# Attention and a two-layer product on one core: bias product for two pairs, bias rows and weights moved in the DMA queues, second matmul from the end of the eighth slot

## Chip, cores and metric

One core of one Trainium2 chip. The time is the device time of one execution in microseconds. Ratios are the mean time of one kernel's fast runs over the mean of the other's fast runs of the same rounds, so not quite the ratio of the medians quoted beside them. For a program on one core, "slow" says only that a run was over 1.5% above the fastest of the same kernel; such runs are named where they matter.

## The reference, cut to what matters

```python
batch, n_heads, seq, head_dim = 8, 8, 576, 64
scores = q @ k.T / sqrt(64)
cum    = cumsum(maximum(s, 0))                      # along the sequence
bias   = minimum(-(cum[:, None] - cum[None, :]), 0)
attn   = softmax(where(causal, -1e9, scores + bias))
x      = concat_heads(attn @ v)                     # 4608 x 512
h      = x @ w_in                                   # 512 -> 2048
out    = (h * clip(h + 3, 0, 6) / 6) @ w_out        # 2048 -> 512
```

## The kernel before

Two heads make a pair, and one turn of the main loop (a **slot**, counted from 0, so the eighth slot is slot 7) handles one of the 32 pairs. From slot 4 on, groups of four matmuls of the two-layer product ("1": first layer, "2": second layer) fill TensorE's time between the parts of the attention. The plan of the first slots is fixed; a dot is an empty place:

```python
NROW = 1                                    # pairs whose bias comes by extra matmuls
plan = list("1.1.1.1" + "1.1.1.1." + "1.1.1.12" + "12121.12")     # slots 4, 5, 6, 7
```

The bias of pair 0 comes by extra matmuls (`picked` holds one selected row set per head). For pairs after that, four bias rows are appended to q and k by a small DMA (`load_aug`), and from pair 8 on also a staircase of constants (`set_stair`, two GpSimd copies). The queue order on GpSimd and SyncE is the order of this loop (cut):

```python
    load_aug(1, nc.sync)
    for i in range(2): load_qk(2, i)        # SyncE, into raws[2]
    load_v(1, nc.sync)
    load_aug(2, nc.sync)
    for i in range(2): load_qk(3, i)
    load_aug(3, nc.sync)
    load_v(2, nc.sync)
    cast_qk(1); cast_v(0); cast_qk(2)       # GpSimd
    ...
    I, U = load_w_in, load_w_out            # GpSimd's DMA queue
    for p in range(NP):
        if NPE <= p + 3 < NP:               # NPE = 9
            for i in range(2): load_qk(p + 3, i)                  # SyncE
        if NPROD <= p + 3 < NPROD + NQK:    # p = 5 .. 8
            set_stair((p + 3) % NQK, nc.gpsimd.tensor_copy)
        if p and p + 3 < NP:
            load_aug(p + 3, nc.gpsimd)
        ...
        elif p:                             # p >= 4
            qk_ahead()                      # GpSimd loads q, k of pairs 7, 8
            if NPE <= p + 2 < NP:
                cast_qk(p + 2)              # GpSimd
                crossbar_qk(p + 2)          # SyncE: DMA transpose into jt
            for fn, c in {4: ((I, 2),), 5: ((U, 0), (U, 1)), 6: ((I, 3),),
                          7: ((U, 2), (U, 3)),
                          8: ((U, 4), (U, 5), (U, 6), (U, 7))}.get(p, ()):
                fn(c)
            if nxt: cast_v(p + 1)           # GpSimd
        if p + 3 < NP: load_v(p + 3, nc.sync)
        # then TensorE, ScalarE, VectorE work of pair p; VectorE spreads jt of pair p + 1
```

The softmax here doesn't subtract the row's maximum and nothing guards it: scores larger than these inputs give would overflow.

## Time and profile before

| | before |
|---|---|
| median of the runs | 380.63 us (379.78 to 381.44) |
| span of the profiled run, mean granted clock | 378.9 us, 0.973 |
| TensorE busy | 354.6 us |
| slot 4, slot 8, slot 9 begin (first score matmul) | 33.01, 71.91, 88.85 us |
| from slot 9 to the end | 290.0 us |

How to read it: TensorE is full from slot 9 on, so the question is only when slot 9 begins. Slot 8 alone lasts 16.9 us, while slots 9 to 11 last some 9.2 us each. The lines that show this stand in the prediction below. (The prediction has slot 9 at 89.02, a time from the chain of work; TensorE's timeline has its first score matmul at 88.85.)

### The profile page before, as it was taken

The page shows a single profiled execution, that of the slowest core. Times are in us where ns is not written, and L with a number is a line of the kernel's source. Part 1 is how long each engine was busy: PE and PEld are TensorE (multiplying, and loading weights), DVE is VectorE, ACT ScalarE, POOL GpSimd, SP SyncE. Part 2 cuts the span into 40 slices and gives each one's busy share as a digit, 9 for nine tenths or more (in the row PEclk, how much of TensorE's full clock was granted, in tenths as well). Part 3 has the DMA queues.
Part 4 walks back from the last instruction along what each step waited for, and adds up shares of the span by engine and source line. Part 5 has one row for each costly group of instructions (what it writes and reads, how often), then busy time and mean ns, then how long its engine had stood idle before and what let it go on. Part 6 is the DMA issues. An engine that isn't in the chain of part 4 may idle for free.

```text
span 378.9 us, 7705 instructions
## 1 busy us (share of the span) xinstructions
PE 354.6 (94%) x2895; PEld 196.1 (52%) x2895; DVE 245.1 (65%) x547; ACT 217.6 (57%) x379; POOL 128.6 (34%) x223
## 2 busy tenths in 40 slices
PE   7879996659998899999999999999999999999996
PEld 3656663335554555555555555555555544444442
DVE  7755984517689776767676767676766644535541
ACT  4646983425665766666666666666666534343420
POOL 5578885523547533333333333333200000000000
PEclk9988999859999999999999999999999999999999
DMA  9799999395998799998999979797921101001102
GB/s 184 145 170 199 213 218 193 49 212 103 222 166 170 156 185 175 189 156 190 156 171 177 209 135 228 129 206 154 197 54 45 47 28 57 36 20 57 57 22 88
DMA packets 158141, 52.76 MB, mean 139 GB/s; under 512 B 146824, under 2 KB 153016, under 8 KB 158104
## 3 DMA queue, kind: packets, MB, share of 16 engines
q1 hardware_dynamic: 148680, 45.64, 60.8%
q0 software_dynamic: 8160, 6.20, 10.6%
q10 hardware_dynamic: 1264, 0.44, 0.6%
q8 instruction: 22, 0.36, 0.4%
q14 instruction: 15, 0.12, 0.1%
HBM read 37.36 MB, written 9.44 MB: 124 GB/s over the span
## 4 chain that ended last, share of the span: by engine, by line
PE 76%; DMA 6%; POOL 6%; issue 5%; DVE 4%; ACT 1%; SPq 1%; POOLq 0%
PE po L466 31%; PE ph L439 29%; PE O L373 6%; PE S L303 6%; PE S L292 3%; DMA w_in_sb<-in_moe_w_in_dram 2%; DMA raw<-in_k_dram 2%; DMA w_out_sb<-in_moe_w_out_dram 2%; POOL qk L140 1%; POOL qk L568 1%; DVE qk L208 1%; DVE gT L455 1%; POOL tok L180 1%; DMA raw<-in_q_dram 1%; POOL va L184 1%
## 5 line engine op out<-in xcount | busy, mean ns | idle before, releaser
L466 PE MATMUL po<-w_out_sb,gT 128*128 128x512 f16 x576 | 147.3, 380 | 9.7 <-DMA w_out_sb<-in_moe_w_out_dram 9.7
L455 DVE SCALAR_TENSOR_TENSOR gT<-tr,ph 128x512 f16<-128x512 f32 x144 | 98.7, 685 | 86.8 <-ACT tr L454 85.7
L439 PE MATMUL ph<-xT,w_in_sb 128*128 128x512 f16 x576 | 149.4, 381 | 1.5 <-DMA w_in_sb<-in_moe_w_in_dram 1.0
L322 ACT ACTIVATE P<-S 128x512 f16<-128x512 f32 x192 | 112.1, 594 | 59.6 <-PE S L292 30.8
L454 ACT ACTIVATE tr<-ph,bias 128x512 f32<-128x512 f32 x144 | 99.0, 687 | 81.9 <-PE ph L439 73.3
L466 PEld LDWEIGHTS <-gT 128*128 128x128 f16 x576 | 50.3, 98 | 56.1 <-issue 11.2
L439 PEld LDWEIGHTS <-w_in_sb 128*128 128x128 f16 x576 | 51.5, 98 | 45.5 <-DMA w_in_sb<-in_moe_w_in_dram 1.1
L140 POOL DMA_DIRECT2D qk<-rows_of x56 | 32.6, 583 | 112.4 <-PE Sc L344 52.8
L303 PE MATMUL S<-qk 68*128 68x448 f16 (+3 forms) x256 | 50.9, 281 | 0.2 <-ACT P L322 0.2
L373 PE MATMUL O<-va,P 128*128 128x65 f16 x896 | 49.3, 196 | 1.1 <-POOL va L184 1.1
L373 PEld LDWEIGHTS <-P 128*128 128x128 f16 x896 | 41.1, 99 | 15.4 <-issue 1.9
L180 POOL CAST tok<-raw 128x576 f16<-128x576 f32 x52 | 33.7, 677 | 14.4 <-DMA raw<-in_q_dram 8.5
L303 PEld LDWEIGHTS <-qk 68*128 68x128 f16 x256 | 24.3, 101 | 25.3 <-issue 2.1
L208 DVE COPY qk<-jt 64x768 f16<-64x768 f16 x92 | 34.6, 376 | 1.3
L396 DVE TENSOR_TENSOR x<-O,rl 128x320 f16<-128x320 f32 x64 | 31.5, 492 | 2.2
L292 PEld LDWEIGHTS <-qk 128*128 128x128 f16 (+1 forms) x256 | 20.2, 100 | 17.8 <-issue 2.9
L475 DVE TENSOR_SCALAR ob<-po 128x512 f32<-128x512 f32 x36 | 24.6, 683 | 7.0 <-PE po L466 7.0
L292 PE MATMUL S<-qk 128*128 128x128 f16 (+1 forms) x256 | 26.0, 223 | 3.1 <-DVE qk L208 2.3
L324 DVE TENSOR_TENSOR P<-P,shut 128x512 f16<-128x512 f16 x48 | 21.4, 445 | 5.4 <-ACT P L322 5.3
L395 DVE RECIPROCAL rl<-O 128x5 f32<-128x5 f32 x64 | 12.1, 189 | 15.1 <-PE Sc L344 8.2
L184 POOL CAST va<-vraw 128x512 f16<-128x512 f32 x32 | 20.1, 628 | 3.2 <-PE O L373 2.6
L238 DVE COPY qk<-pt 64x576 f16<-64x576 f16 x15 | 12.0, 803 | 6.4 <-ACT qk L238 5.1
(69 smaller groups left out, 170.4 us busy)
## 6 DMA issues: line engine op xcount, KB each, us to landing
out_dram<-ob SPq DMA_DIRECT2D x36, 256.0 KB, 2.7
vraw<-in_v_dram SPq DMA_DIRECT2D x64, 128.0 KB, 6.3
raw<-in_q_dram SPq DMA_DIRECT2D x27, 288.0 KB, 4.2
raw<-in_k_dram SPq DMA_DIRECT2D x26, 288.0 KB, 5.9
w_in_sb<-in_moe_w_in_dram POOLq DMA_DIRECT2D x4, 512.0 KB, 8.6
w_out_sb<-in_moe_w_out_dram POOLq DMA_DIRECT2D x8, 256.0 KB, 6.5
vraw<-in_v_dram SPq DMA_DIRECT2D x32, 32.0 KB, 3.0
qk<-rows_of POOLq DMA_DIRECT2D x56, 9.0 KB, 3.2
```

Of the source, the lines that this page charges most:

```text
L140: eng.dma_start(out=qks[p % NQK][64:68, hh, :, 64 * hh : 64 * hh + SEQ], in_=rows_of[g // 32].rearrange("(r g) i t -> g r i t", g=32)[g % ...
L180: copy(out=toks[p][:, c], in_=raws[p % NRAW][:, c])
L208: copies[par](out=qk[0:64, :, i, 128 * par : 128 * par + 256 * n].rearrange("p h (s two c) -> p h s two c", two=2, c=128)[:, :, :, 0, :], ...
L292: mm(S[:, c], lhsT=kT[rows, c], rhs=qT[rows, c], start=(j == 0 and not by_product), stop=(j == 3),)
L303: mm(S[:, c : c + w], lhsT=kT[0:68, 128 * j : 128 * (j + 1)], rhs=qT[0:68, 128 * (j + 1) : SEQ], start=(c == 0), stop=(c != 0 and p >= NROW),)
L322: nc.scalar.activation(out=pt[:, c], in_=S, func=AF.Exp, scale=0.125)
L373: mm(o[:, i, :], lhsT=lhsT, rhs=va[:, hh, j, 0:65], **kw)
L396: nc.vector.tensor_tensor(out=X[p][:, :, hh, :], in0=o[:, :, 0:64], in1=rl.to_broadcast([128, 5, 64]), op=ALU.mult,)
L439: mm(ph, lhsT=w_in_sb[:, kc, ft * 128 : (ft + 1) * 128], rhs=xT[:, kc, n * 512 : (n + 1) * 512], start=(kc == 0), stop=(kc == NKC - 1),)
L454: nc.scalar.activation(out=tr, in_=ph, func=AF.Relu, bias=bias3[:, 0:1])
L455: nc.vector.scalar_tensor_tensor(out=gTs[n][:, ft, :], in0=tr, scalar=6.0, in1=ph, op0=ALU.min, op1=ALU.mult)
L466: mm(po, lhsT=gTs[n][:, ft, t4 * 128 : (t4 + 1) * 128], rhs=w_out_sb[:, ft, :], start=(ft == 0), stop=(ft == NFT - 1),)
```

## The change

The intent is to get the weights of the second layer in before TensorE wants them, and to want them a little later. Cut to its core:

```diff
-    NROW = 1
+    NROW = 2
-    picked = keep("picked", [128, 2, SEQ], F16)
+    picked = w_out_sb.rearrange("p f j -> p (f j)")[:, 0 : 2 * NROW * SEQ].rearrange(...)
-    plan = list("1.1.1.1" + "1.1.1.1." + "1.1.1.12" + "12121.12")
+    plan = list("1.1.1.1" + "1.1.1.1." + "1.1.1.1." + "1.1.1212")
+    (rows 64 to 67 of pair 1's q and k zeroed by two ScalarE multiplications)
     # front
-    load_aug(1, nc.sync)          # also load_aug(2), load_aug(3)
     cast_qk(1)
+    load_aug(2, nc.gpsimd)
     cast_v(0)
     cast_qk(2)
+    load_aug(3, nc.gpsimd)
+    cast_v(1)
     # loop
-        if NPROD <= p + 3 < NPROD + NQK:
-            set_stair((p + 3) % NQK, nc.gpsimd.tensor_copy)
-        if p and p + 3 < NP:
-            load_aug(p + 3, nc.gpsimd)
                 4: ((I, 2),),
-                5: ((U, 0), (U, 1)),
-                6: ((I, 3),),
-                7: ((U, 2), (U, 3)),
-                8: ((U, 4), (U, 5), (U, 6), (U, 7)),
+                5: ((I, 3),),
+                6: ((U, 0), (U, 1), (U, 2), (U, 3)),
+                7: ((U, 4), (U, 5), (U, 6), (U, 7)),
             ...
+            if NPROD <= p + 2 < NPROD + NQK:
+                set_stair((p + 2) % NQK, nc.gpsimd.tensor_copy)
+            if p + 2 < NP:
+                load_aug(p + 2, nc.gpsimd)
     # slots 2, 3: load_aug(4), load_aug(5) go last; cast_v(3) one slot later, cast_v(4) ahead of qk_ahead()
     # bias of the second half of the heads: each step one slot later
```

Below, "front" means the bias product for pair 1 and all that moves ahead of the loop; "plan" the later second matmuls; "weights" all the rest in the loop. Slots are counted from 0 here; the "slot eight" in the name of the prediction's step 4 is the eighth one, slot 7.

More of the change, by code (lines that the diff above doesn't have):

```diff
@@ L95 @@
     sel = keep("sel", [128, 4], F32)
-    picked = keep("picked", [128, 2, SEQ], F16)
+    picked = w_out_sb.rearrange("p f j -> p (f j)")[:, 0 : 2 * NROW * SEQ].rearrange(
+        "p (g t) -> p g t", t=SEQ
+    )
     toks = {}
@@ L539 @@
     load_v(0, nc.sync)
-    for i in range(NROW):
-        fill(nc.gpsimd, qks[i][64:68, :, :, :], 0.0)
     fill(nc.gpsimd, ident, 0.0)
@@ L591 @@
     fill(nc.gpsimd, rows_of[0][:, 1, SEQ:640], 0.0)
+    fill(nc.gpsimd, qks[0][64:68, :, :, :], 0.0)
+    for hh in range(2):
+        nc.scalar.mul(
+            out=qks[1][64:68, hh, :, 64 * hh : 64 * hh + 640],
+            in_=rows_of[0][64:68, 0, None, :].to_broadcast([4, 2, 640]),
+            mul=0.0,
+        )
     for i in range(NQK):
@@ L665 @@
     load_v(1, nc.sync)
-    load_aug(2, nc.sync)
     for i in range(2):
         load_qk(3, i)
-    load_aug(3, nc.sync)
     load_v(2, nc.sync)
     cast_qk(1)
+    load_aug(2, nc.gpsimd)
     cast_v(0)
     cast_qk(2)
+    load_aug(3, nc.gpsimd)
+    cast_v(1)
     for i in range(2):
@@ L694 @@
         if p == 1:
-            cast_v(1)
             cast_qk(3)
@@ L700 @@
             qk_ahead()
+            load_aug(4, nc.gpsimd)
+        elif p == 3:
             cast_v(3)
-        elif p == 3:
             load_w_in(1)
+            cast_v(4)
             qk_ahead()
-            cast_v(4)
+            load_aug(5, nc.gpsimd)
         elif p:
@@ L724 @@
             nc.sync.dma_start(out=stair_sb, in_=stair_dram.ap())
-        if p == 9:
+        if p == 10:
             load_s(1, (nc.sync,) * 4)
             fill(nc.gpsimd, rows_of[1][:, 0, :], 1.0)
-        if p == 10:
+        if p == 11:
             cum1(1, nc.gpsimd)
-        if p == 11:
+        if p == 12:
             cum2(1)
             nc.gpsimd.tensor_copy(out=rows_of[1][0:32, 0, 0:SEQ], in_=C["c"][0:32])
-        if p == 12:
+        if p == 13:
             cum3(1, nc.gpsimd)
             cum4(1, nc.gpsimd)
-        if p == 12:
+        if p == 13:
             cum5(1, nc.gpsimd)
```

## The prediction

> **What bounds the kernel now.** I read the page's engine shares and slices first, then TensorE's waits, then the chain that ended last, and then the timelines of TensorE and GpSimd where the chain leaves TensorE. The shares and slices:
>
> ```profile
> PE 354.6 (94%) x2895; PEld 196.1 (52%) x2895; DVE 245.1 (65%) x547; ACT 217.6 (57%) x379; POOL 128.6 (34%) x223
> ...
> PE   7879996659998899999999999999999999999996
> ...
> PEclk9988999859999999999999999999999999999999
> DMA  9799999395998799998999979797921101001102
> GB/s 184 145 170 199 213 218 193 49 212 103 222 166 170 156 185 175 189 156 190 156 171 177 209 135 228 129 206 154 197 54 45 47 28 57 36 20 57 57 22 88
> ```
>
> The reader should see that TensorE is full from slice 10 on (about 90 us) and has nothing left to give there. Nearly all its idle time (378.9 - 354.6 = 24.3 us) lies in the first 90 us, together with two stretches of lowered clock. The eighth slice moves only 49 GB/s while its neighbours move 193 and 212: DMA stood empty there although the kernel was short of weights. Who was waited for, by TensorE between 60 and 90 us:
>
> ```profile
> PE po L466 <- DMA w_out_sb<-in_moe_w_out_dram: 9.7, 4, 5.9
> ```
>
> and why those weights came late, in GpSimd's timeline:
>
> ```profile
> 58.62 1.47 POOL L156 DMA_DIRECT2D w_out_sb<-in_moe_w_out_dram  x2
> ...
> 62.46 1.25 POOL L568 COPY qk<-stair_sb 64x1280 f16<-64x1280 f16 x1 [1.52 <-PE Sc L344]
> 70.20 1.25 POOL L568 COPY qk<-stair_sb 64x1280 f16<-64x1280 f16 x1 [6.48 <-PE S L303]
> 71.40 1.20 POOL L140 DMA_DIRECT2D qk<-rows_of  x2
> 72.64 1.37 POOL L180 CAST tok<-raw 128x576 f16<-128x576 f32 x2
> 73.96 2.88 POOL L156 DMA_DIRECT2D w_out_sb<-in_moe_w_out_dram  x4
> ```
>
> This is a loop. The last four weight transfers stand behind a staircase copy in GpSimd's in-order queue; the copy waits for TensorE to finish with a pair's buffer; TensorE itself stands waiting for earlier weights (third and fourth transfers, issued at 58.62). So the last weights start at 73.96 and TensorE stands again. TensorE's timeline, with the early wait as well:
>
> ```profile
> 23.74 0.57 PE L222 MATMUL pt<-ident,tok 128*128 128x128 f16 x5 [1.51 <-POOL tok L180]
> ...
> 65.35 0.65 PE L466 MATMUL po<-w_out_sb,gT 128*128 128x512 f16 x2 [1.82 <-DMA w_out_sb<-in_moe_w_out_dram]
> ...
> 78.25 1.01 PE L466 MATMUL po<-w_out_sb,gT 128*128 128x512 f16 x2 [5.94 <-DMA w_out_sb<-in_moe_w_out_dram]
> 80.66 1.01 PE L466 MATMUL po<-w_out_sb,gT 128*128 128x512 f16 x2 [1.40 <-DMA w_out_sb<-in_moe_w_out_dram]
> ```
>
> **What the Trainium skill says.** "TensorE: Matmul & The Clock Gate", Part 1, says that idleness drops TensorE to half clock until some 3.4 us of work have passed. The trace agrees in kind: after 23.74 the starts of successive 512-column matmuls go from 0.22 to 0.43 us apart until 31.6; the same from 65.8 to 69.2 and from 80.7 to 86.7. So a removed wait is worth more than itself. "DMA: Bandwidth & Descriptors", section "Issuing engines are not separate DMA queues", says that transfers of all issuers interleave on the same 16 engines, so issuing weights earlier gives no extra bandwidth, only fills holes; the 49 GB/s slice is such a hole. "SBUF — State Buffer", the list of practical consequences under who interferes with whom, says that a VectorE copy in a two-port mode and a GpSimd instruction lock each other out. The trace agrees: the two query/key copies of VectorE that take 0.67 us at 104.67 take 3.30 us at 115.15, beside GpSimd's bias casts. That matters for the part of the change that shifts the second bias by one slot.
>
> **The change part by part.** A slot is one head pair; slot 4 begins at 33.01, slot 7 at 56.72, slot 8 at 71.91, slot 9 at 89.02 (the starts of each pair's first score matmuls).
>
> (1) Bias product for a second pair. Pair 1 gets its bias by extra matmuls instead of by rows sent by DMA. For pair 0 these cost three groups of 0.22 us a head (spacing of the starts at 13.43, 14.09 and 14.78 to the next group) plus 0.03 in the corner: 0.69 a head, 1.38 for pair 1, all on TensorE: **+1.4 us**. The two further picks on VectorE (0.36 each) end near 11.9, and VectorE was idle 0.98 before its next copy at 12.18: nothing. Two ScalarE multiplications of 1280 columns fall between the table load's end at 3.43 and the first cast at 5.93, which waited 2.5 us for its data. From the 0.67 us of a 576-column cast and 0.70 of a 768-column copy I estimate 1.1 to 1.3 each, so they end at 5.7 to 6.0: at most 0.1. The picked rows now lie in the second weights' memory; the first such weights arrive 20 us after their last use: nothing.
>
> (2) Bias rows leave SyncE's queue. SyncE stood from 7.81 to 9.27 waiting for the rows, and later again, so pair 2's load started at 10.62 and pair 3's at 15.39. Now they can go at about 7.9 and 11.4. GpSimd's cast of pair 3 waited 2.81 us for k and ended at 23.68, which gave TensorE's 1.51 wait; by bytes (about 3.3 MB ahead of it at some 175 GB/s) it should land near 18 to 19. Two waits for value casts (0.64 at 19.42, 0.49 at 26.25) go as well, since those casts move ahead. **-2.6 us**, and the half-clock stretch from 25.0 to 31.6 (6.6 less 0.5 idle, half of it lost) **-3.1 us**. The row transfers now cost GpSimd 1.2 us per pair between casts, where it has room.
>
> (3) Weights ahead of staircases, staircases one slot later. The staircase for pair p+2 goes into a buffer whose pair ended a slot before, so the 6.48 us stall of GpSimd goes and the loop is cut. By adding GpSimd's durations in the new order I expect the last first-matmul weights near 35 (they were at 50.3), second weights 0 to 3 at 37 to 40 (44.3 and 58.6), 4 to 7 at 46 to 49 (74.0). With 6.5 to 9 us of landing these are there by 58. This removes 9.74 of waits for second weights, 0.99 for first weights (at 58.57), and the half-clock losses of 65.8 to 69.2 (1.7) and 80.66 to 86.69 (0.4 in the two matmuls, 2.5 after): **-15.3 us**.
>
> (4) Second matmul from the end of slot eight. Walking through the plan and the rules that follow it, two groups of four matmuls (0.86 us each) leave slots 6 and 7 and fall into slot 8, where first matmuls are not ready and four places were empty. From slot 9 to the end both kernels do the same groups in the same places, with 12 left for the tail. Same work: 0, but weights are wanted some 2 us later.
>
> (5) Second half's bias one slot later. The waits of 1.75, 0.33, 0.42 and 0.22 between 116 and 128 may move by a slot, but I see no reason for them to go or grow much: 0.
>
> Sum: 380.6 + 1.4 - 2.6 - 3.1 - 15.3 = 361.0.
>
> **The rivals.** *DMA becomes the bound of the front.* Up to the last second weights (80.6) the core moved some 13.85 MB; its best stretch (48.6 to 56.7) ran at 221 GB/s at a share of 1.24. About 13.0 MB of that is needed by them or before. With 3.5 MB in the first 20 us and 215 GB/s after, the end is at 20 + 9.5/0.215 = 64 us. TensorE, by my new starts (slot 4 at 29, slot 8 at 61, slot 9 at 69), wants weights 4 and 5 near 65 and 6 and 7 near 68. That is a tie, not a margin. For it: DMA is already full from 27 to 56. Against it: the order is weights first, and v and raw loads are three pairs ahead. If it wins, waits of 3 to 8 us with some half clock come back: 365 to 370.
>
> *A wait on the first weights or rows takes the place of the early one.* First weights chunk 0 would be issued at 20 and land at 28.6 by the median of 8.6; slot 4 wants them at 29.9. The rows of pair 4 (issued near 22.3, 5.5 us landing early on) are wanted at 29.2, the q and k of pair 4 at 26.5. Each is within 1 or 2 us. Likely cost 0 to 3, up to 5 with a clock drop: 361 to 366.
>
> *The gain is given back later*, through collision of the shifted bias work on GpSimd with VectorE's copies, or since slots 12 and 13 have seven empty places: 0 to 3 us more.
>
> I add **2.5 us** to the sum for the first two together: **363.5 us**.
>
> **Range and chances.** The low end, 358.5, is the sum with no new wait and a little from the waits near 116 to 128. The high end, 371, is the DMA rival in full with an early wait. For not being faster by over 2% the time must stay above 373.0, so more than 12 of the 22.4 us gained gross would have to return; the change moves transfers only to earlier places in time and adds 1.4 us of work, so I give that 7 in 100: faster 0.93, same 0.06, slower 0.01.
>
> **What would show it right or wrong.** Right: second-weight transfers all issued before 52; TensorE's wait for them under 1 us; no 49 GB/s hole; clock above 0.98 (0.973 before); TensorE idle near 12 us and busy near 348; slot 9 starting near 69 to 72. Step 2 is wrong if TensorE still waits for a token cast near 21 or its clock falls before 32. Step 3 is wrong if GpSimd waits several us elsewhere ahead of the weights, say for a landing of v or raw. If DMA is the bound, weights are issued early but land over 12 us later. Step 4 is wrong if the number of second-matmul groups in the tail is not 12. The prediction fails altogether if a new wait over 5 us stands on TensorE before 90 us.

## The result, and the profile after

The changed kernel takes 368.8 us in median (366.3 to 369.8, 4 runs) against 381.0 of the kernel before (the three runs above and one of 384.1); the ratio is 0.966 (0.958 to 0.973). Predicted were 363.5, with 358.5 to 371 as the range. So the direction and the range held, and 5.3 us of the predicted gain did not come. The page of the profiled run, its lines that answer to those of before:

```profile
PE 351.6 (96%) x2913; PEld 194.1 (53%) x2913; DVE 251.0 (68%) x549; ACT 219.4 (60%) x381; POOL 133.7 (36%) x227
...
PE   8997999599998999999999999999999999999995
...
PEclk9999999899998999999999999999999999999999
DMA  9999999998898687989799979797521101101111
GB/s 183 211 203 212 205 193 161 172 214 184 194 183 175 154 190 167 189 136 211 160 192 181 189 165 185 169 191 159 123 77 20 57 2 57 57 2 58 57 57 60
```

The hole of 49 GB/s is gone, and the DMA engines are full from the first slice to the ninth. TensorE has one deep dip left, in the eighth slice, and a shallow one in the fourth. Whom it waited for up to 95 us (total, times, longest):

```profile
PE O L375 <- DVE x L398: 4.0, 1, 4.0
...
PE S L294 <- DMA qk<-rows_of: 0.8, 1, 0.8
```

No wait for second weights remains. In place of 9.7 us there is one wait of 4.0, put down to a VectorE instruction. VectorE's timeline shows what that instruction stood behind, and the chain that ended last shows the way back (start, length, what):

```profile
63.39 0.69 DVE L326 TENSOR_TENSOR P<-P,shut 128x512 f16<-128x512 f16 x1
69.22 0.66 DVE L210 COPY qk<-jt 64x768 f16<-64x768 f16 x2 [5.14 <-DMA jt<-tok]
69.80 0.18 DVE L397 RECIPROCAL rl<-O 128x5 f32<-128x5 f32 x1
70.02 0.49 DVE L398 TENSOR_TENSOR x<-O,rl 128x320 f16<-128x320 f32 x1
```

```profile
35.56 18.75 DMA raw<-in_q_dram
54.31 0.05 issue
54.36 1.28 POOL tok L182 x2
55.64 0.02 issue
55.66 13.54 DMA jt<-tok
```

Read from the top: the q of pair 9 was asked for at 35.56 and took 18.75 us to land, GpSimd cast it at 54.36, SyncE issued its DMA transpose at 55.66, and this took 13.54 us more. VectorE stood for the transposed tile from 64.08 to 69.22, and the normalisation behind it in its queue (L397, L398), which frees what TensorE needs next, came at 69.80 and 70.02. So the wait has two ingredients: a late transpose, and VectorE's order, in which the copies for pair 9 stand ahead of the normalisation of pair 7. Only the first was worked on below. With the two swapped, the normalisation need not have waited, and the tile that landed at 69.20 would have been copied out by about 70.6 (two pairs of copies, 0.66 us a pair: an estimate from these lines), ahead of the 70.97 at which slot 9 begins in the fastest profile below. No run tests this. GpSimd issued the last four weight transfers in the same microsecond as the transpose, since they too stood behind the cast:

```profile
42.08 2.88 POOL L158 DMA_DIRECT2D w_out_sb<-in_moe_w_out_dram  x4 [1.75 <-DMA qk<-rows_of]
...
54.36 1.27 POOL L182 CAST tok<-raw 128x576 f16<-128x576 f32 x2 [4.90 <-DMA raw<-in_q_dram]
55.58 2.88 POOL L158 DMA_DIRECT2D w_out_sb<-in_moe_w_out_dram  x4
```

Slot by slot, from the first score matmul of each pair:

| begin of | before | predicted | after |
|---|---|---|---|
| slot 4 | 33.01 | 29 | 28.67 |
| slot 8 | 71.91 | 61 | 61.89 |
| slot 9 | 88.85 | 69 | 75.81 |
| end, counted from slot 9 | 290.0 | as before | 290.8 |

All but one entry fit within 1 us. The shortfall is slot 8: it lasts 13.9 us where the sum had some 8. Its row in the table of stretches (stretch, length, then busy time and count for TensorE, weight loads, VectorE, ScalarE, GpSimd; clock, DMA share, GB/s) is this for the kernel before (cut at 89.02), then for the changed one:

```profile
71.91:89.02 17.11, 9.57 (x73) 5.68 (x72) 6.64 (x17) 4.22 (x8) 7.98 (x14) 0.70 0.78 133
```

```profile
61.89:75.81 13.92, 9.79 (x79) 5.23 (x77) 6.08 (x17) 4.37 (x8) 9.85 (x15) 0.88 1.22 161
```

DMA share went from 0.78 to 1.22 (it adds up the times of all packets, so it passes 1 where they overlap). Before, the engines had idle time in this slot; after, transfers lie on top of each other. It is not bytes alone: this slot moves 161 GB/s, while slot 9 of the same run moves 221 at a share of 0.99.

### The profile page after: what moved, and what is told of

It is laid out like the page before. It is cut to its first block, busy times and chain, and to the rows that moved or that the text cites. A ratio compares the mean times of both kernels' runs of the same rounds, so it can differ in the third digit from the quotient of the medians.

```text
span 366.6 us, 7736 instructions
## 1 busy us (share of the span) xinstructions
PE 351.6 (96%) x2913; PEld 194.1 (53%) x2913; DVE 251.0 (68%) x549; ACT 219.4 (60%) x381; POOL 133.7 (36%) x227
## 4 chain that ended last, share of the span: by engine, by line
PE 77%; DMA 12%; DVE 5%; POOL 2%; issue 1%; SPq 1%; ACT 1%; POOLq 0%; DVEq 0%; ACTq 0%
PE po L468 32%; PE ph L441 30%; PE O L375 6%; PE S L305 6%; DMA raw<-in_q_dram 5%; DMA jt<-tok 4%; PE S L294 3%; DMA vraw<-in_v_dram 2%; DMA raw<-in_k_dram 2%; DVE qk L210 1%; DVE gT L457 1%; DVE c L623 1%; POOL tok L114 1%; POOL tok L182 1%; SPq L134 0%
## 5 line engine op out<-in xcount | busy, mean ns | idle before, releaser
L182 POOL CAST tok<-raw 128x576 f16<-128x576 f32 x52 | 36.7, 710 | 107.6 <-DMA raw<-in_q_dram 98.2
L375 PE MATMUL O<-va,P 128*128 128x65 f16 x896 | 48.4, 194 | 4.0 <-DVE x L398 4.0
L305 PE MATMUL S<-qk 68*128 68x448 f16 (+3 forms) x256 | 49.5, 274 | 0.2
L375 PEld LDWEIGHTS <-P 128*128 128x128 f16 x896 | 40.1, 98 | 18.1 <-DVE x L398 4.3
L210 DVE COPY qk<-jt 64x768 f16<-64x768 f16 x92 | 38.2, 415 | 6.5 <-DMA jt<-tok 5.1
L142 POOL DMA_DIRECT2D qk<-rows_of x60 | 35.2, 589 | 1.4 <-DMA w_in_sb<-in_moe_w_in_dram 1.4
L398 DVE TENSOR_TENSOR x<-O,rl 128x320 f16<-128x320 f32 x64 | 31.5, 492 | 2.4 <-DVE rl L397 0.2
L326 DVE TENSOR_TENSOR P<-P,shut 128x512 f16<-128x512 f16 x48 | 22.3, 465 | 4.5 <-ACT P L324 4.4
L397 DVE RECIPROCAL rl<-O 128x5 f32<-128x5 f32 x64 | 12.0, 188 | 7.2 <-PE O L375 7.1
```

Of the source, the lines that this page charges most:

```text
L142: eng.dma_start(out=qks[p % NQK][64:68, hh, :, 64 * hh : 64 * hh + SEQ], in_=rows_of[g // 32].rearrange("(r g) i t -> g r i t", g=32)[g % ...
L182: copy(out=toks[p][:, c], in_=raws[p % NRAW][:, c])
L210: copies[par](out=qk[0:64, :, i, 128 * par : 128 * par + 256 * n].rearrange("p h (s two c) -> p h s two c", two=2, c=128)[:, :, :, 0, :], ...
L305: mm(S[:, c : c + w], lhsT=kT[0:68, 128 * j : 128 * (j + 1)], rhs=qT[0:68, 128 * (j + 1) : SEQ], start=(c == 0), stop=(c != 0 and p >= NROW),)
L375: mm(o[:, i, :], lhsT=lhsT, rhs=va[:, hh, j, 0:65], **kw)
L398: nc.vector.tensor_tensor(out=X[p][:, :, hh, :], in0=o[:, :, 0:64], in1=rl.to_broadcast([128, 5, 64]), op=ALU.mult,)
```

## The experiments

Two questions: which part brought the 12 us, and what is the 4 us wait that remains made of? Each run was timed beside the kernel before on the same chip. All gave correct results. By the 2% rule the verdict is "same" for d_front_only and "unclear" for d_plan_only and d_front_plan_only, "faster" for the rest; every interval lies below 1. The table collects the runs of the first question, with the begin of slot 9 in each profile and the waits of TensorE for second weights.

| run | parts of the change in it | median us | ratio to before (95%) | slot 9 | wait for second weights |
|---|---|---|---|---|---|
| before | none | 380.63 | 1 | 88.85 | 9.7 |
| d_front_only | front | 377.81 | 0.988 (0.984 to 0.991) | 84.95 | 10.6 |
| d_plan_only | plan | 374.84 | 0.981 (0.976 to 0.986) | 81.98 | 4.7 |
| d_weights_only | weights | 371.61 | 0.971 (0.965 to 0.976) | 80.70 | 4.4 |
| d_front_plan_only | front, plan | 371.53 | 0.975 (0.969 to 0.981) | 77.99 | 5.0 |
| d_front_undone | plan, weights | 370.85 | 0.968 (0.961 to 0.975) | (slow profile) | |
| d_plan_old | front, weights | 368.89 | 0.966 (0.959 to 0.972) | 75.63 | none |
| changed kernel, again | all | 369.04 | 0.968 (0.964 to 0.971) | 75.01 | none |

### Undoing one part: d_front_undone, d_front_plan_only, d_plan_old

d_front_undone puts the front back: `NROW = 1`, `load_aug(1..3, nc.sync)`, `cast_v(1)` in slot 1, the rest as changed.

> The changed kernel with its front put back: bias product for pair 0 only, bias rows of pairs 1 to 3 sent by SyncE, value cast of pair 1 in slot 1. Theory A (the changed kernel is held in slot 8 by the late transpose of pair 9, which landed at 69.2 us after a chain of transfers, not of TensorE work): TensorE comes to slot 8 some 3 to 4 us later and waits that much less there, so 368 to 371 us. Theory B (the parts add up as the prediction summed them): the front was worth 4.3 us, so 372.5 to 374 us with a wait of some 4 us still in slot 8.

Measured 370.85 (367.3 to 373.5; its profile fell in a slow run and is not used). The ratio, 0.968 (0.961 to 0.975), cannot be told from that of the changed kernel (0.966 and 0.968). A loss of 4.3 us would have given about 0.977, just beyond the interval's end, so theory A fits better. With the other two parts there, the front brought 0 to 1 us as measured; by the two intervals, a loss of up to some 3 us against the control is not excluded.

d_front_plan_only is the kernel before with the front and the plan; weights and staircases stay in the old order.

> The kernel before with only the new front and the new plan of second matmuls; weights and staircases stand in the old order. If the loop of weights, staircase and TensorE decides when TensorE gets past slot 8, the front's 4.3 us (7.1 before the product's 1.4 and so on) mostly vanish in longer waits for second weights: 378 to 381 us, waits for second weights 8 to 12 us. If parts add up: 375 to 377 us, waits for second weights about 9.7 us less 1 to 2 for the later start.

Measured 371.53, ratio 0.975: some 4 us better than even the additive expectation, which had given the plan nothing. TensorE waits half as long for second weights although their order is the old one:

```profile
PE po L468 <- DMA w_out_sb<-in_moe_w_out_dram: 5.0, 2, 3.2
```

d_plan_old is the changed kernel with the one line of the plan put back.

```diff
-    plan = list("1.1.1.1" + "1.1.1.1." + "1.1.1.1." + "1.1.1212")
+    plan = list("1.1.1.1" + "1.1.1.1." + "1.1.1.12" + "12121.12")
```

> The changed kernel with the old plan (second matmuls from the end of slot 6). Second weights 0 to 3 were issued at 42.1 to 45.0 and land within 11 us, so by 54 to 56, while the old plan wants them from 51.5 on. Theory A: up to 2 us of new wait for weights in slots 6 and 7, which the wait in slot 8 gives back, so 368 to 370 us. Rival: the waits add to the slot-8 wait with another clock drop, 371 to 374 us.

Measured 368.89, ratio 0.966, the same as the changed kernel. No wait for weights came up in slots 6 and 7; the only large one is again slot 8's, 3.4 us. So the plan is worth nothing measurable when front and weights are there, and something large when the weights are in the old order. That asked for each part alone.

### Each part alone: d_plan_only, d_front_only, d_weights_only

> The kernel before with only the new plan of second matmuls. Theory D (the loop of weights, staircase and TensorE can be cut in more than one place, so the parts overlap): with no second matmul in slot 7 that wants the late weights 2 and 3, the waits of 0.58 and 1.82 us and the half clock after them go, TensorE frees the staircase's buffer some 5 us earlier and the last weights are issued near 68 instead of 74: 374 to 377 us. Prediction's step 4 (the plan is worth nothing by itself): 380 to 382 us.

Measured 374.84, ratio 0.981: the expectation of overlapping parts. One line of Python is worth 7 us of 381 by itself. The last four weight transfers go out at 68.97 instead of 73.96, with not one GpSimd instruction moved:

```profile
68.97 2.89 POOL L156 DMA_DIRECT2D w_out_sb<-in_moe_w_out_dram  x4
```

> The kernel before with only the new front. Theory D: the front shifts the whole loop earlier by its own 4 us, so 376 to 378 us with the waits for second weights near 9 us as before. If the loop were tied to the arrival of weights alone: 380 to 381 us with longer waits.

Measured 377.81, ratio 0.988, as expected: slot 9 begins 3.9 us earlier, and the waits for second weights stay:

```profile
PE po L468 <- DMA w_out_sb<-in_moe_w_out_dram: 10.6, 4, 5.8
```

> The kernel before with only the new order of weights, staircases, bias rows and second bias. Theory D: it cuts the loop by itself, so it takes most of the gain: 369 to 372 us, with up to 2 us of waits for second weights since the old plan wants them early. If the parts add up (front 4.3 us): 373 to 374 us.

Measured 371.61, ratio 0.971, within the expected 369 to 372, with a wait of 4.4 us (up to 2 had been expected). Alone the three parts gain some 5, 7 and 11 us, 23 together (1 minus the ratio, times 381); combined they gain 12 to 13. The loop that the prediction found can be cut at TensorE's end (ask later, so that TensorE frees the staircase's buffer sooner) or at GpSimd's end (send the weights first). Either cut takes most of what the other would.

### What the remaining wait is made of: e_raw9_early, after_again, e_u_ahead, e_raw9_slot5, e_both

e_raw9_early asks for q and k of pair 9 two slots sooner; their buffer had been free since 19.4 us.

```diff
-        if NPE <= p + 3 < NP:
+        if NPE < p + 3 < NP:
             for i in range(2):
                 load_qk(p + 3, i)
+        if p == 4:
+            for i in range(2):
+                load_qk(NPE, i)
```

> The changed kernel with the q and k of pair 9 loaded by SyncE at the start of slot 4 instead of slot 6 (same bytes, earlier in the queue). Theory A (order): they took 18.8 us to land at 54.3; asked for before v of pairs 7 and 8 they land by 45, the cast, the last second weights and the transpose follow some 6 us earlier, the wait of 4 us in slot 8 and its half clock (1.8 us) go: 362.5 to 365 us. Rival C (bandwidth: the front of the kernel is bound by bytes or packets whatever their order): the wait moves to another load and the time stays within 367 to 370 us.

Measured 362.5, 363.8, 365.3 and 369.9 us (the last counted slow), ratio of the fast runs 0.953 (0.947 to 0.958): the expected time. In the profiled run TensorE has no wait over 1.2 us anywhere and slot 9 begins at 70.97. But the way there was not the one expected. The cast of pair 9 and the weights came not earlier but 2.5 us later, since GpSimd now stood for v of pair 7, which had been put behind:

```profile
52.00 0.61 POOL L186 CAST va<-vraw 128x512 f16<-128x512 f32 x1 [6.99 <-DMA vraw<-in_v_dram]
...
56.82 1.27 POOL L182 CAST tok<-raw 128x576 f16<-128x576 f32 x2
58.03 2.88 POOL L158 DMA_DIRECT2D w_out_sb<-in_moe_w_out_dram  x4
```

What differs is the transpose. It was issued at 58.12, again beside the weights, and no transpose of this run up to 90 us took over 6.1 us, where the changed kernel's took up to 13.5 (the last line of the view of the tile jt: least, median and most from issue to landing, first the changed kernel, then this run):

```profile
DMA to landing us min/median/max: 5.3/5.6/13.5
```

```profile
DMA to landing us min/median/max: 4.7/5.6/6.1
```

So the gain goes with a fast transpose and not with an earlier cast, and the weights in the same microsecond are not enough to make it slow. With the slow run counted in, the mean ratio would still be 0.957. To see whether the weights or SyncE's own loads made the transpose slow, four more ran on one chip with five rounds: the changed kernel as a control, and three orders. The early load itself was not among them.

> The changed kernel unaltered, as a control beside the three below on the same chip: 366 to 370 us, ratio to before near 0.966, the wait of 3 to 4 us in slot 8 for the transpose of pair 9 in the profile.

The control gave 369.04 (367.7 to 370.1), ratio 0.968, with a wait of 3.4 us in slot 8 and the transpose again slow (11.8 us).

e_u_ahead sends the last four weights ahead of pair 9's cast:

```diff
+            if p == 7:
+                for c in range(4, 8):
+                    load_w_out(c)
             if NPE <= p + 2 < NP:
                 cast_qk(p + 2)
                 crossbar_qk(p + 2)
-                7: ((U, 4), (U, 5), (U, 6), (U, 7)),
```

> The changed kernel with the last four second-weight transfers ahead of the cast of pair 9 on GpSimd (they waited behind it for pair 9's load until 55.6; now issued near 49.5). Theory W (pair 9's transpose took 13.5 us to land because these weights were issued in the same microsecond): it lands within 7 us of its issue near 57, the wait goes, 363 to 365 us. Theory Q (it stood behind SyncE's own backlog, v of pair 8 and q, k of pair 10 issued just before it): it still takes 10 us or more, and pair 9's load is delayed further by the weights; 367 to 370 us.

Measured 363.8, 365.4, 368.5, 369.4, 369.5 and 369.9, median 368.98: no clear gain (the ratio of 0.960 counts only the three fastest, since the others lie 1.5% above the best). Two of the six runs were as fast as the early load's (clock 0.998 and 0.995), as one of the early load's was slow (0.990), so the wait may come and go between executions; one execution of each is profiled. In it the transpose was fast, 6.2 us (no transpose up to 90 us took over 7.0). But pair 9's k now landed later, and the transpose could only be issued at 60.24:

```profile
50.04 2.90 POOL L158 DMA_DIRECT2D w_out_sb<-in_moe_w_out_dram  x4
...
58.11 0.67 POOL L182 CAST tok<-raw 128x576 f16<-128x576 f32 x1 [3.82 <-DMA raw<-in_k_dram]
```

In its profiled run 2.8 us of wait remained in slot 8. What the transpose gained, the load before it lost.

The eight fast profiles that have the "weights" part can be compared in this one transfer, the transpose of pair 9. It took 11.8 to 14.1 us in six of them (changed kernel twice, d_plan_old, d_weights_only, and e_raw9_slot5 and e_raw9_pair1rows below). In each of the six, SyncE had finished issuing k of pair 10 at most 0.6 us before, and the four weights were issued within 2 us of the transpose. It took 6.0 in the early load (k of pair 10 issued 3.2 us before, weights beside it) and 6.2 in e_u_ahead (k just before, weights 10 us before). So in these runs a slow transpose goes with both neighbours at once and with neither alone. With one run for each exception this is a pattern and not a shown cause.

> The early load of pair 9 at the start of slot 5 instead of slot 4, so behind v of pair 7 and ahead of v of pair 8. GpSimd's 7 us wait for v of pair 7 should go, the cast of pair 9 come near 49 to 52 and the last weights follow: 362 to 365 us, as with slot 4. If the load needs the full three transfers' head start, its cast stays past 54 and the wait in slot 8 stays over 2 us: 366 to 369 us.

Measured 370.68 (367.7 to 372.1), ratio 0.973: no gain, as the second expectation had it, and slower than its 366 to 369. GpSimd stood 4.26 us for k of pair 9, cast it at 53.66, and the wait in slot 8 was 4.6:

```profile
53.66 0.67 POOL L182 CAST tok<-raw 128x576 f16<-128x576 f32 x1 [4.26 <-DMA raw<-in_k_dram]
```

> The early load of pair 9 in slot 4 and the weights ahead of its cast. If the value cast of pair 7, which GpSimd waited 7 us for with the early load, stands behind the weights no more, nothing on TensorE changes, since no wait of TensorE hung on it: 362 to 365 us, as with the early load alone. If the weights issued near 56 now meet the transfers of v for pair 7 and of pair 10: 365 to 368 us.

Measured 367.4 to 373.2, median 371.53, ratio 0.970: worse than the early load alone, outside the expected 362 to 365 us. Its profile fell in a slow run, so where it waited is not told from it.

What follows: between slots 4 and 8 of the changed kernel (28.67 to 61.89) the DMA share lies at 1.13 to 1.26 and the rate at 178 to 209 GB/s, so a transfer that is moved ahead puts others back. Of four ways to reorder the same bytes, three left the time within 1% of the changed kernel's; in two of these GpSimd's wait for k of pair 9 took the place of what was saved, and for e_both it is not known. The fourth, the early load in slot 4, was faster in its one set of rounds (0.953, up to 0.958, against 0.968, from 0.964, of the control and 0.966, from 0.958, of the changed kernel's first set) and is the fastest version here; it was not run a second time, and e_both, which contains it, was not fast. Whether 364 us would hold on another chip is open.

### What the bias product for pair 1 is worth: e_raw9_pair1rows

The early-load kernel, with pair 1's bias by rows from SyncE again:

```diff
-    NROW = 2
+    NROW = 1
+    load_aug(1, nc.sync)
     for i in range(2):
         load_qk(2, i)
     load_v(1, nc.sync)
```

> The kernel with the early load of pair 9, and pair 1's bias by rows sent by SyncE again instead of the product (the rest of the new front stays). If the product costs its 1.4 us of TensorE work and the rows come in time: 362 to 363 us. If the rows come late (they can be sent from 8.6 us on, took 5.5 us to land in median, and pair 1 begins at 14.5) or the loads behind them in SyncE's queue shift by 1 us or more: 364 to 367 us with a new wait of TensorE in slots 1 to 3.

Measured 370.47 (367.8 to 372.4), ratio 0.968 against 0.953, above both expected ranges. The rows of pair 1 came in time. But SyncE stood for them, and pair 2's q, issued at 8.09 in the changed kernel, went out at 10.22:

```profile
8.85 1.32 SPq L140 DMA_DIRECT2D qk<-rows_of  x2
10.22 0.44 SPq L117 DMA_DIRECT2D raw<-in_q_dram  x1
```

All later loads shifted with it, GpSimd stood for v three times by 33 us, and the rows of pair 4 reached TensorE late:

```profile
32.11 0.59 PE L292 MATMUL S<-qk 68*128 68x128 f16 x4 [3.31 <-DMA qk<-rows_of]
```

The wait in slot 8 came back as well, 3.5 us, with a transpose of 14.1 us. So the 1.4 us of extra TensorE work buy a head start of 2 us for everything that SyncE sends. Its worth in this pair of kernels was 6 us; given the spread of the early-load kernel, read it as "more than its cost", not as 6.

## Why the prediction was right or wrong, point by point

**What bounds it**: right. Everything is decided before slot 9. In all twelve fast profiles the stretch after slot 9 is 289.4 to 290.9 us.

**Step 1, the product, +1.4**: right in size. Slot 1 lasted 4.26 us without its wait before (15.21 to 20.11 less 0.64), and 5.47 after (14.51 to 19.98): +1.2. The ScalarE multiplications took 2.42 us together and ended at 5.85, ahead of the cast that they could have held up.

**Step 2, the front**: right in mechanism and size. The cast of pair 3 came at 18.78 (predicted 18 to 19), the wait for it went, the clock stayed full, and slot 4 began at 28.67 (predicted 29). Alone it moved slot 9 by 3.9 us (the step's net with the product was 4.3). What the step did not say is that the gain can be lost again further on: with plan and weights there, d_front_undone measures 0 to 1 us. That slot 8's wait for a transpose takes up the difference, as theory A had it, is not shown, for its profile is a slow one. Where that wait is gone, in the early-load kernel, undoing a part of the front cost some 6 us.

**Step 3, the weights, -15.3**: the waits for second and first weights went as predicted, and weights 0 to 3 were issued at 42.1 (predicted 37 to 40). The last four were issued at 55.6, not 46 to 49; the check that the prediction named ("all issued before 52") failed. The mis-sized term is the landing of pair 9's load: the sum added up GpSimd's durations with no wait in it, but the load took 18.75 us and GpSimd stood 4.90 us for it. The prediction had named just this as the sign against step 3, a wait of several us for a landing of v or raw.

**Step 4, the plan, 0**: wrong as a statement about the part. Alone it is worth 7 us, since it lets TensorE be done with the staircase's buffer sooner; that it adds nothing measurable to front and weights is what d_plan_old shows. The sum came out near right because the credit due to it stood under step 3, and that is luck in part. Its own check holds: 12 groups are left for the tail (48 matmuls in 10.60 us in both profiles).

**The rival of DMA as the bound, and the 2.5 us for new waits**: the rival named the right resource and was undersized in the sum. It watched the weights; the transfer that came late was another one, the transpose of pair 9, which the prediction never timed. In slot 8 it cost 3.99 us of wait and, by the spacing of the matmuls from 71.1 to 74.9 (0.43 instead of 0.22 us a matmul of 512 columns), 1.7 us of half clock: 5.7 us. The late rows of pair 4 added 0.75 (slot 4, predicted as one of three near misses). Together 6.4 against the 2.5 allowed. The rival's own sign, weights that land over 12 us after their issue, did not come: the most was 11.0.

**The prediction's argument against that rival**, "v and raw loads are three pairs ahead", failed for pair 9: asked for three pairs ahead in program order, its q landed only 18.75 us later.

**Step 5, second bias, 0**: nearly. The wait that stood at 116 to 118 in the kernel before (1.75) is now at 110 to 112 (1.24 and 0.19), and a stretch of half clock followed it, 112.3 to 116.1. The part after slot 9 is 0.8 us longer, but that cannot be put down to this step: it is 290.7 in d_front_only, which lacks the step, and 289.7 in d_plan_old, which has it.

**Other signs and readings**: of the signs named, the hole of 49 GB/s went and the clock rose to 0.988 (above 0.98 was asked), but slot 9 began at 75.81 and not at 69 to 72, and TensorE was busy for 351.6 us and idle for 15.0, not 348 and 12. Three readings in the prediction are off without touching its sum. Of the idle time before, 17.5 of 24.3 us lay ahead of 89.02, which is not nearly all. The gross gain was 21.0 us (2.6 + 3.1 + 15.3), not 22.4. And beside the 3.30 us of VectorE copies at 115.15 GpSimd ran casts of q, k and v; its bias cast began only at 117.64.

## What to carry to other kernels

When a late transfer sits in a loop (a transfer behind a copy, the copy behind a buffer, the buffer behind the engine that waits for the transfer), look for every place where the loop can be cut, and do not add up the gains of the cuts: here three parts gained 5, 7 and 11 us alone and 12 to 13 together. Once the loop is cut and the DMA engines are full, list every transfer that the next stage needs and time the slowest one, the transposes too, for a median landing time says little then (5.6 us was the median where the one that counted took 13.5). Look also at what stands behind the waiting copy in its engine's queue. A little extra work on the busy engine can be cheap if it takes a wait out of the head of a DMA queue.

## What the Trainium skill lacked or had wrong

- "DMA: Bandwidth & Descriptors", section "Issuing engines are not separate DMA queues", calls the time to initiate a DMA usually small beside the DMA itself. Here it was not always: one issue of k of pair 9 in the changed kernel held SyncE's queue for 5.80 us, about a third of the 16.5 us until the load landed; the median for an issue of k in this run was 0.73.
- The same page, in its section on the anatomy of one DMA, gives a fixed part and a part by bytes for transfers that GpSimd issues. It has no landing times for transfers that share full engines. Here the 256 KB weight transfers that GpSimd issued took 6.1 to 11.0 us, SyncE's loads of 288 KB up to 90 us took 4.0 to 18.8, and its transposes between 50 and 80 us took 5.3 to 13.5.
- "TensorE: Matmul & The Clock Gate", the table of why this matters, warns of idle gaps over about 3 us. Here half clock followed a gap of 1.51 us at 22 to 24 (with shorter ones near it) in the kernel before and gaps of 1.24 and 0.19 at 110 to 112 in the changed one, while the gap of 1.75 at 117 to 118 in the kernel before was followed by full clock. In these two profiles the length of the gap alone did not tell.
